# Sliding-window attention and adapter router: the transpose of the attention result by DMA instead of by TensorE and VectorE

## The chip, the cores and the metric

The kernel runs on one core of a Trainium2 chip. The metric is the device time of one execution in microseconds (us). The engines are PE (TensorE: matmuls; its weight loads are shown as PEld), ACT (ScalarE), DVE (VectorE), POOL (GpSimd) and SP (SyncE). POOL and SP do little here but issue DMAs, POOL the loads and SP the stores; 16 DMA engines move the data of both.

## The reference

q, k and v are float32 of shape 8 batches x 8 heads x 576 positions x 64. Each position attends to the positions at a distance of at most 32 in its own head. The result, laid out as 4608 rows of 512, is the input x of a router over 8 experts with adapters of rank 16; the best two experts add their adapter's output to the row.

```
scores = scale * np.matmul(q, k.transpose(0, 1, 3, 2))
mask = np.abs(pos[:, None] - pos[None, :]) <= window          # window = 32
attn = softmax(np.where(mask, scores, -1e9))                  # abridged
x = matmul(attn, v).transpose(0, 2, 1, 3).reshape(B * S, H * D)
...
logits = x @ w_gate                                           # K = 2 best of 8
for e in range(E):
    z = x[mask] @ A[e]                                        # 512 -> 16
    delta[mask] += w[mask, k, None] * (z @ B[e])              # 16 -> 512
return x + delta
```

## The kernel before, in words

Everything on the chip between the loads and the output is float16, with sums in float32 in PSUM. The unit of the attention is a pair of heads of one batch: 4 pairs a batch, 32 units u in all, each cut into 9 blocks of 64 keys. Eight blocks make one tile T of scores, 36 tiles in all.

Per batch b, the stages are these, each a small function named by two letters:

- LD and LV (L286, L290) load q, k (six loads) and v (two), issued by POOL, which casts them to float16 on the way. RG (L301) regroups q and k by a DVE copy; SV (L295) does v's.
- TR (L306) transposes q and k on PE, eight small matmuls against the identity for each of six pieces; EQ and EK (L315, L321) evict them by ACT.
- SC(T) (L328) computes a tile of scores into PSUM: two matmuls that write the mask and eight of q and k. EX(T) (L341) takes the exponential by ACT. PV(u) (L346) multiplies by v, 13 matmuls, with a column of ones that gives the sum. MU(u) (L359) divides by the sum on DVE: a reciprocal (L364) and a multiplication (L365) into the buffer x of the batch, 128 partitions x 5 groups x 512.
- When the four units of a batch are done, x must lie transposed. TX(b, h) (L372) does that on PE: 20 transposes of 128 x 128, in three parts h of 8, 8 and 4, into the PSUM buffers T. XE(b, h) (L381, the copy is L383) copies each part into xT on DVE.
- PZ(b) (L387, the matmul is L391) multiplies xT with the router's weights and all adapters' A, 20 matmuls. G1, GA, G2 (L400 to L431) pick the two best experts and scale on DVE, with one small exponential on ACT. TZ (L433) transposes the scaled result on PE and ZE (L439) evicts it on ACT.
- PD(b, h) (L443) forms the output in PSUM for the three parts h (256, 256 and 128 positions): the adapters' B (L446) plus x itself, by multiplying xT with the identity (L449). OB(b, h) (L453) evicts it to a float32 buffer ob, by ACT (L458) for h = 0 and 1 (128 x 1024) and by DVE (L460) for h = 2 (128 x 512). ST(b, h) (L462, the issue is L466) stores it from SP.

Buffers: x and xT have two copies each (NX, NXT), ob three (NOB), v three (NV), the raw loads seven pieces each of q and k (NRAW). PSUM is divided into three buffers W of 128 x 1024 float32 (NW; SC, PV, PZ and PD take them) and two buffers T of 128 x 1024 float16 (NTP; TR, TX and TZ take them).

The order of the instructions on every engine is fixed at build time. `tasks` (L64) lists each stage with its engine, its cost in us, what it depends on and which PSUM buffer it takes; every stage has a due time, counted in units u, which is its unit plus a number from the table OFF (L58). `plan` (L169) then places the tasks one by one in modelled time: on each engine, among the tasks that can start within `horizon` of the earliest, the one with the smallest due time. Loads have the engine "DMA" and stores the engine "DMO", and share one modelled transfer time; a task that depends on a load or a store waits `lat` (2.0 us) more. The kernel emits the stages in that order (L523) and keeps it (`keep` is the call that holds an instruction to its place in the program). At run time an engine works through its list in order and waits at each instruction for what it needs.

Of the kernel before, what the change touches and what calls it, by code (L numbers as in the profile page):

```python
# [16 lines left out]
B, H, S, D = 8, 8, 576, 64  # L17
E, R, DD = 8, 16, 512
ER = E * R
NP = H // 2  # L20
# [18 lines left out]
NV, NPT, NRAW, NCAST, NX, NXT, NOB = 3, 4, 7, 3, 2, 2, 3  # L39
# [9 lines left out]
class Task:  # L49
# [3 lines left out]
    def __init__(self, key, eng, cost, deps, take=None, give=None, lat=0.2):  # L53
# [1 line left out]
        self.take, self.give, self.lat = take, give, lat  # L55


OFF = {"LD": -10.16, "LV": -7.58, "RG": -2.51, "TR": -3.5, "EQ": -0.91, "EK": 8.24, "SV": 11.71,  # L58
       "SC": -2.02, "EX": 9.98, "PV": -0.24, "MU": -0.5, "TX": 0.38, "XE": -20.72, "PZ": 4.91,
       "G1": -40.48, "GA": 17.51, "G2": -27.59, "TZ": -20.47, "ZE": 17.82, "PD": 10.1, "OB": -2.95,  # L60
       "ZK": -28.38, "ZV": 29.47, "ZP": 16.04}


def tasks(off=OFF):  # L64

    ts = {}

    def add(key, u, eng, cost, deps, take=None, give=None, lat=0.2):
        t = Task(key, eng, cost, [d for d in deps if d in ts], take, give, lat)
        t.due = u + off[key[0]]  # L70
        t.seq = len(ts)
        ts[key] = t

    for i in range(2):
        for o in (0, 1):
            add(("ZK", i, o), -4.0 + 8 * i, "DVE", 1.05, [])
    for i in range(NPT):
        add(("ZP", i), -3.0 + i, "DVE", 0.56, [])
    for i in range(NV):
        for o in (0, 1):  # L80
            add(("ZV", i, o), 4 * i, "ACT" if i == 1 else "DVE", 2.2 if i == 1 else 1.2, [])

    def tiles_of(b):
        return range(NS * b // TB, (NS * b + NS - 1) // TB + 1)

    for b in range(B + 1):
        u0 = NP * b
        if b < B:
            for t in range(NT3):
                for w in (0, 1):  # L90
                    i = NT3 * b + t - NRAW
                    add(("LD", b, w, t), u0 + 1.333 * t, "DMA", 1.15,
                        [("RG", i // NT3, w, i % NT3)], lat=2.0)
            for o in (0, 1):
                add(("LV", b, o), u0 + o, "DMA", 1.8,
                    [("PV", NP * (b - NV) + n) for n in range(NP)], lat=2.0)
            for t in range(NT3):
                u = u0 + 1.333 * t
                for w in (0, 1):
                    i = NT3 * b + t - NCAST  # L100
                    add(("RG", b, w, t), u, "DVE", 0.43,
                        [("LD", b, w, t), ("TR", i // NT3, w, i % NT3)])
                for w in (0, 1):
                    add(("TR", b, w, t), u, "PE", 0.42, [("RG", b, w, t)], take="T")
                old = [("SC", T) for T in tiles_of(b - 2)] if b > 1 else []
                add(("EQ", b, t), u, "ACT", 0.80, [("TR", b, 0, t)] + old,
                    give=("TR", b, 0, t))
                add(("EK", b, t), u, "ACT", 1.60, [("TR", b, 1, t)] + old,
                    give=("TR", b, 1, t))
            for o in (0, 1):  # L110
                add(("SV", b, o), u0, "DVE", 0.78, [("LV", b, o)])

        for T in range(NT):
            last = TB * T + TB - 1
            if last // NS != b:
                continue
            need = set()
            for blk in range(TB * T, TB * T + TB + 1):
                bb, s = divmod(blk, NS)
                if bb < B and blk <= last:  # L120
                    need |= {("EQ", bb, s // BT), ("EK", bb, s // BT)}
                    if s % NB != NB - 1:
                        need.add(("EQ", bb, (s + 1) // BT))
                    need |= {("ZK", bb % 2, 0), ("ZK", bb % 2, 1)}
            u = (TB * T) / NB
            add(("SC", T), u, "PE", 0.90, list(need), take="W")
            pold = [("PV", v) for v in range(NU)
                    if NB * v < TB * (T - NPT) + TB and NB * v + NB > TB * (T - NPT)]
            add(("EX", T), u, "ACT", 1.03, [("SC", T)] + pold, give=("SC", T))
        us = [u for u in range(NU)  # L130
              if (NB * u + NB - 1) // TB in [T for T in range(NT) if (TB * T + TB - 1) // NS == b]]
        for u in us:
            bb = u // NP
            add(("PV", u), u, "PE", 0.80,
                [("EX", T) for T in range(NB * u // TB, (NB * u + NB - 1) // TB + 1)]
                + [("ZP", T % NPT) for T in range(NB * u // TB, (NB * u + NB - 1) // TB + 1)]
                + [("SV", bb, 0), ("SV", bb, 1), ("ZV", bb % NV, 0), ("ZV", bb % NV, 1)],
                take="W")
            add(("MU", u), u, "DVE", 1.05,
                [("PV", u)] + [("TX", bb - NX, h) for h in range(3)], give=("PV", u))  # L140
            if u % NP != NP - 1:
                continue
            v0 = NP * bb
            for h in range(3):
                n = 2 if h < 2 else 1
                add(("TX", bb, h), v0, "PE", 0.23 * n,
                    [("MU", v0 + i) for i in range(NP)], take="T")
                add(("XE", bb, h), v0, "DVE", 0.68 if n == 2 else 0.42,
                    [("TX", bb, h)] + [("PD", bb - NXT, i) for i in range(3)],
                    give=("TX", bb, h))  # L150
            add(("PZ", bb), v0, "PE", 1.2, [("XE", bb, h) for h in range(3)], take="W")
            add(("G1", bb), v0, "DVE", 1.08, [("PZ", bb)])
            add(("GA", bb), v0, "ACT", 0.22, [("G1", bb)])
            add(("G2", bb), v0, "DVE", 1.95, [("GA", bb)], give=("PZ", bb))
            add(("TZ", bb), v0, "PE", 0.30, [("G2", bb)], take="T")
            add(("ZE", bb), v0, "ACT", 0.70, [("TZ", bb)], give=("TZ", bb))
            for h in range(3):
                n = 2 if h < 2 else 1
                add(("PD", bb, h), v0 + 0.8 * h, "PE", 0.45 * n, [("ZE", bb)], take="W")
                k = 3 * bb + h - NOB  # L160
                add(("OB", bb, h), v0 + 0.8 * h, "ACT" if h < 2 else "DVE",
                    1.02 if n == 2 else 0.70, [("PD", bb, h), ("ST", k // 3, k % 3)],
                    give=("PD", bb, h))
                off["ST"] = off["OB"]
                add(("ST", bb, h), v0 + 0.8 * h, "DMO", 0.5 * n, [("OB", bb, h)], lat=2.0)
    return ts


def plan(off=OFF, horizon=0.036):  # L169

    ts = tasks(off)
    for t in ts.values():
        t.users, t.start = [], None
# [10 lines left out]
    n = len(ts)  # L184
    while len(order) < n:
# [45 lines left out]
        if t.give:  # L231
            g = ts[t.give]
# [11 lines left out]
def kernel(  # L244
# [10 lines left out]
    nc = tc.nc  # L255
    keep = tc.keep_in_program_order
# [6 lines left out]
    def many(n, shape, dt, name):  # L263
        return [const.tile(shape, dt, name=f"{name}{i}") for i in range(n)]
# [7 lines left out]
    xs = many(NX, [128, NG, DD], F16, "x")  # L272
    xTs = many(NXT, [128, NG, 4, 128], F16, "xT")
# [4 lines left out]
    Ts = [psum.tile([128, 1024], F16, name=f"T{i}") for i in range(NTP)]  # L278

    ts, order = plan()  # L280

    def ps(*key):
        t = ts[key]
        return (Ws if t.take == "W" else Ts)[t.slot]
# [96 lines left out]
    def XE(b, h):  # L381
# [2 lines left out]
            out=xTs[b % NXT][:, 2 * h:2 * h + n].rearrange("p g c k -> p (g c k)"),  # L384
            in_=ps("TX", b, h)[:, 0:512 * n]))

    def PZ(b):  # L387
        xT, pz = xTs[b % NXT], ps("PZ", b)
        for g in range(NG):
            for c in range(4):  # L390
                keep(nc.tensor.matmul(out=pz[:, GS * g:GS * g + ER + E],  # L391
                                 lhsT=xT[:, g, c, :], rhs=WA_sb[:, c, :],
                                 start=(c == 0), stop=(c == 3)))
# [68 lines left out]
    def ST(b, h):  # L462
        for i, g in enumerate(gs(h)):
# [1 line left out]
            r0 = S * b + 128 * g - 32  # L465
            keep(nc.sync.dma_start(out=out[r0 + lo:r0 + hi], in_=obs[(3 * b + h) % NOB][lo:hi, i]))  # L466

    do = dict(LD=LD, LV=LV, SV=SV, RG=RG, TR=TR, EQ=EQ, EK=EK, SC=SC, EX=EX, PV=PV, MU=MU,
              TX=TX, XE=XE, PZ=PZ, G1=G1, GA=GA, G2=G2, TZ=TZ, ZE=ZE, PD=PD, OB=OB, ST=ST)


# [92 lines left out]
```

## Time and profile before

| | us |
|---|---|
| three runs | 149.59, 150.68, 153.41 (median 150.68) |
| the profiled execution | 148.89 |
| its span, first to last instruction | 146.7 |
| busy: PE, ACT, DVE, POOL | 119.8, 116.3, 113.3, 51.9 |
| granted TensorE clock, mean | 0.979 |
| read from and written to HBM | 28.85 MB, 9.44 MB |

The views of the profile used below are: the page's slices, which cut the span into 40 equal parts and show the busy share of each in tenths; busy time by stretch, a row for each stretch of the span with the busy us of each engine and the number of its instructions; the groups by shape, with the line, engine and operation, the tiles written and read, the count, then busy us in all, ns of one, and after the second bar the engine's idle time just ahead of such instructions with what ended it; the waits, which name the waiting engine and line, then what it waited for, us in all, the number of times and the longest; the timeline, instructions in order with start and duration, and in brackets the idle time ahead; the chain of waits that ended last, with start, us and what; and the DMA issues, with the median us from issue to landing. An "L" with a number is a line of the kernel.

### The profile page before, as it was taken

The numbers are of one execution on the slowest core, as the hardware profiler recorded it, in microseconds if no ns is written. First come the engines' busy times: TensorE is split into PE (matmuls) and PEld (weight loads), VectorE is DVE, ScalarE is ACT, GpSimd is POOL, SyncE is SP. The second block draws the span as 40 slices with busy tenths as digits, with TensorE's granted clock in tenths as the row PEclk, the third lists the DMA queues.
The fourth block names the chain that finished last, engine by engine and source line by source line (L and its number), as shares of the span: only waits on it lengthen the run. The fifth ranks groups of instructions, "written<-read, shape, count | busy, mean of one in ns | idle before, by whom it ended". The sixth has DMA issues, their size and how long they took to land.

```text
span 146.7 us, 4230 instructions
## 1 busy us (share of the span) xinstructions
PE 119.8 (82%) x1720; PEld 100.8 (69%) x1720; DVE 113.3 (77%) x284; ACT 116.3 (79%) x143; POOL 51.9 (35%) x79
## 2 busy tenths in 40 slices
PE   0179779859889989878999999999999999693550
PEld 0156667649768978667789888997898788582330
DVE  6897899578997999975999999979738775967110
ACT  7789969948998899749999799989998994433150
POOL 7995657984576726610491044000000000000000
PEclk9999999999999999999999999999999999999686
DMA  2999999999999999999999959990542023058035
GB/s 20 179 157 179 196 191 95 163 150 180 205 191 194 225 226 195 235 264 241 257 177 206 249 104 125 227 238 8 197 179 93 0 58 130 0 201 290 32 136 186
DMA packets 38771, 24.13 MB, mean 164 GB/s; under 512 B 24800, under 2 KB 34144, under 8 KB 38752
## 3 DMA queue, kind: packets, MB, share of 16 engines
q0 software_dynamic: 33504, 14.43, 89.8%
q1 hardware_dynamic: 5248, 9.44, 18.6%
q8 instruction: 13, 0.21, 0.6%
q14 instruction: 6, 0.05, 0.1%
HBM read 28.85 MB, written 9.44 MB: 261 GB/s over the span
## 4 chain that ended last, share of the span: by engine, by line
PE 38%; DMA 21%; ACT 15%; DVE 11%; issue 6%; POOL 5%; SPq 0%; ACTq 0%; POOLq 0%; DVEq 0%
DMA vbd<-in_v_dram 12%; PE W L355 6%; ACT kT L325 5%; PE W L331 5%; DMA l<-in_q_dram 5%; ACT PT L342 5%; PE W L337 5%; PE W L446 5%; PE W L449 5%; DMA out_dram<-ob 4%; PE T L377 4%; PE W L391 4%; POOL l L288 3%; PE T L311 3%; ACT qT L317 3%
## 5 line engine op out<-in xcount | busy, mean ns | idle before, releaser
L342 ACT ACTIVATE PT<-W 128x1024 f16<-128x1024 f32 x36 | 36.9, 1025 | 6.3 <-PE W L337 5.4
L325 ACT COPY kT<-T 64x768 f16<-64x768 f16 x48 | 38.1, 794 | 1.7 <-PE T L311 1.3
L311 PE MATMUL T<-ident,c 96*128 96x96 f16 x384 | 24.0, 213 | 9.9 <-DVE c L303 8.0
L355 PE MATMUL W<-vbd,PT 128*128 128x130 f16 x416 | 29.1, 219 | 1.7 <-DVE vbd L298 0.8
L311 PEld LDWEIGHTS <-c 96*128 96x128 f16 x384 | 20.0, 101 | 11.7 <-DVE c L303 9.6
L365 DVE TENSOR_TENSOR x<-W,rc 128x640 f16<-128x640 f32 x32 | 26.4, 825 | 1.1
L355 PEld LDWEIGHTS <-PT 128*128 128x128 f16 x416 | 25.2, 97 | 2.2 <-issue 2.2
L337 PEld LDWEIGHTS <-kT 128*128 128x128 f16 x288 | 19.5, 99 | 9.2 <-issue 0.8
L458 ACT COPY ob<-W 128x1024 f32<-128x1024 f32 x16 | 16.1, 1012 | 9.5 <-PE W L449 6.0
L331 PE MATMUL W<-ident,mask 128*128 128x512 f16 x72 | 22.1, 390 | 1.5 <-DVE x L365 0.8
L303 DVE COPY c<-l 96x1024 f16<-96x1024 f16 x48 | 20.3, 450 | 3.3 <-DMA l<-in_q_dram 2.3
L293 POOL DMA_DIRECT2D vbd<-in_v_dram x16 | 13.5, 846 | 25.5 <-PE W L355 17.5
L337 PE MATMUL W<-qT,kT 128*128 128x128 f16 x288 | 22.5, 221 | 0.0
L317 ACT COPY qT<-T 128x768 f16<-128x768 f16 x24 | 19.1, 797 | 3.3 <-PE T L311 3.2
L288 POOL DMA_DIRECT2D l<-in_k_dram x24 | 15.8, 658 | 6.0 <-DVE rc L364 2.6
L288 POOL DMA_DIRECT2D l<-in_q_dram x24 | 16.2, 673 | 3.6 <-POOLq L548 0.9
L449 PEld LDWEIGHTS <-xT 128*128 128x128 f16 x160 | 12.9, 102 | 6.0 <-issue 1.5
L446 PE MATMUL W<-B_sb,zT 128*128 128x512 f16 x40 | 16.0, 400 | 1.2 <-ACT zT L440 0.8
L449 PE MATMUL W<-ident,xT 128*128 128x128 f16 x160 | 16.2, 226 | 0.0
L383 DVE COPY xT<-T 128x1024 f16<-128x1024 f16 (+1 forms) x24 | 13.7, 596 | 3.1 <-PE T L377 3.0
L377 PE MATMUL T<-ident,x 128*128 128x128 f16 x160 | 12.2, 219 | 2.3 <-DVE xT L383 1.8
L298 DVE COPY vbd<-vbd 32x2304 f16<-32x2304 f16 x16 | 12.3, 767 | 1.6 <-DMA vbd<-in_v_dram 1.2
(46 smaller groups left out, 113.1 us busy)
## 6 DMA issues: line engine op xcount, KB each, us to landing
out_dram<-ob SPq DMA_DIRECT2D x24, 256.0 KB, 4.2
l<-in_q_dram POOLq DMA_DIRECT2D x24, 192.0 KB, 8.6
l<-in_k_dram POOLq DMA_DIRECT2D x24, 192.0 KB, 8.9
vbd<-in_v_dram POOLq DMA_DIRECT2D x16, 288.0 KB, 9.0
out_dram<-ob SPq DMA_DIRECT2D x16, 192.0 KB, 3.7
WA_sb<-in_moe_A_dram POOLq DMA_DIRECT2D x4, 32.0 KB, 8.5
B_sb<-in_moe_B_dram POOLq DMA_DIRECT2D x1, 128.0 KB, 4.4
WA_sb<-in_moe_w_gate_dram POOLq DMA_DIRECT2D x1, 8.0 KB, 5.3
```

Source lines behind the costliest of these rows:

```text
L288: keep(nc.gpsimd.dma_start(out=raw[w][(NT3 * b + t) % NRAW], in_=src[FT * t:FT * t + FT]))
L303: keep(nc.vector.tensor_copy(out=cst[w][i % NCAST], in_=raw[w][i % NRAW].rearrange("p o (j d) -> p j o d", j=J)))
L311: keep(nc.tensor.matmul(out=tp[:, FT * slot:FT * slot + FT], lhsT=src[:, j, :], rhs=ident[0:FT, 0:FT], is_transpose=True, start=True, stop ...
L317: keep(nc.scalar.copy(out=qTs[b % 2][:, c0:c0 + J * FT].rearrange("p (f j) -> p f j", j=J), in_=ps("TR", b, 0, t)[:, 0:J * FT].rearrange(" ...
L325: keep(nc.scalar.copy(out=dst.rearrange("p a (r f j) -> p a r f j", r=2, j=4), in_=kt[64 * o:64 * o + 64]))
L331: keep(nc.tensor.matmul(out=p[:, i:i + 4], lhsT=maskT, rhs=bcast(ident, 1, 4), start=True, stop=False))
L337: keep(nc.tensor.matmul(out=p[:, i], lhsT=kTs[b % 2][:, NB * n + a, :], rhs=qTs[b % 2][:, c0:c0 + 128], start=False, stop=(i % 4 == 3)))
L342: keep(nc.scalar.activation(out=PTs[T % NPT][:, :, 64:192], in_=ps("SC", T).rearrange("p (i c) -> p i c", c=128), func=AF.Exp, scale=1.0 / ...
L355: keep(nc.tensor.matmul(out=po[:, GS * g:GS * g + 2 * VD], lhsT=PTs[T % NPT][:, sl, off:off + 128], rhs=rhs[:, :, V0 - 1:V0 + D], start=(i ...
L365: keep(nc.vector.tensor_tensor(out=xs[b % NX].rearrange("p g (h n d) -> p g h n d", h=2, n=NP)[:, :, :, n], in0=pog[:, :, :, 1:VD], in1=bc ...
L446: keep(nc.tensor.matmul(out=pd[:, i], lhsT=zTs[b % 2][:, g], rhs=B_sb, start=True, stop=False))
L449: keep(nc.tensor.matmul(out=pd[:, i, 128 * c:128 * c + 128], lhsT=xTs[b % NXT][:, g, c], rhs=ident, start=False, stop=(c == 3)))
```

## The change

For batches 0 to 6 the new stage XD replaces TX and XE: one DMA transpose, issued by SP, from the batch's buffer x to xT, both in SBUF. Batch 7 keeps TX and XE. XD goes into the plan as a task of the store queue with a cost of 2.6 us and the usual 2.0 us of latency; it depends on the four MU of its batch and on the PD of the batch two before, whose xT it overwrites. PZ depends on it, and so does MU two batches later, which overwrites x. In odd batches the eviction OB with h = 1 goes to DVE. The table OFF is new and horizon is 0, so that all engines' orders differ from before. The lines of XD, and of OB and the rest of the plan:

```
-            add(("MU", u), ..., [("PV", u)] + [("TX", bb - NX, h) for h in range(3)], give=("PV", u))
+            add(("MU", u), ..., [("PV", u)] + [("XD", bb - NX)], give=("PV", u))
...
+            if bb < B - 1:
+                add(("XD", bb), v0, "DMO", 2.6, [("MU", v0 + i) for i in range(NP)]
+                    + [("PD", bb - NXT, i) for i in range(3)], lat=2.0)
-            for h in range(3):
+            for h in range(3 if bb == B - 1 else 0):
                 n = 2 if h < 2 else 1
                 add(("TX", bb, h), ...)
                 add(("XE", bb, h), ...)
-            add(("PZ", bb), v0, "PE", 1.2, [("XE", bb, h) for h in range(3)], take="W")
+            add(("PZ", bb), v0, "PE", 1.2, [("XE", bb, h) for h in range(3)] + [("XD", bb)],
+                take="W")
...
-                add(("OB", bb, h), v0 + 0.8 * h, "ACT" if h < 2 else "DVE",
-                    1.02 if n == 2 else 0.70, ...)
+                add(("OB", bb, h), v0 + 0.8 * h, "ACT" if h < 2 - bb % 2 else "DVE",
+                    0.59 if n == 1 and h < 2 else 1.02 if h < 2 - bb % 2
+                    else 0.69 * n - 0.15 * (n - 1), ...)
...
-def plan(off=OFF, horizon=0.036):
+def plan(off=OFF, horizon=0):
...
+    def XD(b):
+        keep(nc.sync.dma_start_transpose(
+            out=xTs[b % NXT].rearrange("p g c k -> p (g c) k"),
+            in_=xs[b % NX].rearrange("p g c -> p (g c)")))
```

In the table OFF, of the stages around the change: PZ goes from 4.91 to -18.38, G1 from -40.48 to -46.69, G2 from -27.59 to -18.4, TZ from -20.47 to -7.62, PD from 10.1 to 14.0, OB (and with it ST) from -2.95 to 4.96, SC from -2.02 to 1.86, TR from -3.5 to -11.98, MU from -0.5 to -4.43; XD has -15.21.

## The prediction

> **What bounds the kernel now.** I read the clock and the DMA queues first, then the busy time by stretch, then the groups by shape, the waits and the timeline.
>
> ```profile
> PEclk9999999999999999999999999999999999999686
> DMA  2999999999999999999999959990542023058035
> ...
> q0 software_dynamic: 33504, 14.43, 89.8%
> q1 hardware_dynamic: 5248, 9.44, 18.6%
> ```
>
> The clock is full until the tail. q0, the loads that POOL issues, keeps the 16 DMA engines occupied to about 97 us; q1, the stores that SP issues, is light.
>
> ```profile
> core 0: us, PE busy (x) PEld busy (x) DVE busy (x) ACT busy (x) POOL busy (x), PEclk, DMA share, GB/s
> 20.00:30.00 10.00, 7.75 (x119) 6.42 (x118) 7.55 (x16) 8.79 (x12) 7.36 (x11) 1.00 3.20 143
> 70.00:80.00 10.00, 9.86 (x150) 8.46 (x149) 9.40 (x20) 9.93 (x13) 5.66 (x8) 1.00 1.33 211
> 80.00:90.00 10.00, 9.66 (x154) 8.47 (x152) 9.49 (x28) 9.21 (x14) 3.27 (x4) 1.00 1.02 166
> 90.00:100.00 10.00, 9.93 (x163) 8.86 (x161) 8.87 (x26) 9.40 (x13) 0.00 (x0) 1.00 1.06 194
> 130.00:140.00 10.00, 6.02 (x64) 4.38 (x62) 4.22 (x15) 3.27 (x5) 0.00 (x0) 0.85 0.42 145
> ```
>
> Three stages. To about 36 us nothing is full but the DMA. From 70 to 100 us PE is busy 29.45 of 30 us (98.2%), ACT 28.54 (95.1%), DVE 27.76 (92.5%): three engines nearly level, PE ahead. After 130 us the last batch's serial chain leaves all of them idle half the time.
>
> ```profile
> 26.39 0.82 DVE L365 TENSOR_TENSOR x<-W,rc 128x640 f16<-128x640 f32 x1
> 28.71 0.42 DVE L303 COPY c<-l 96x1024 f16<-96x1024 f16 x1 [1.50 <-DMA l<-in_q_dram]
> ...
> 44.72 0.75 DVE L298 COPY vbd<-vbd 32x2304 f16<-32x2304 f16 x1 [0.79 <-DMA vbd<-in_v_dram]
> ...
> 100.05 0.82 DVE L365 TENSOR_TENSOR x<-W,rc 128x640 f16<-128x640 f32 x1
> ...
> 127.76 0.82 DVE L365 TENSOR_TENSOR x<-W,rc 128x640 f16<-128x640 f32 x1
> ```
>
> The 4th L365 (batch 0 finished) starts at 26.39 us, the 32nd (batch 7) at 127.76: seven steps of 14.48 us. A gain per step counts seven times. Loads still hold DVE up at 28.71 and last at 44.72; later it is the other way round, POOL waits for a free V buffer (next fence, 17.5 us in two waits).
>
> ```profile
> POOL vbd L293 <- PE W L355: 17.5, 2, 9.0
> ...
> ACT ob L458 <- DMA out_dram<-ob: 3.5, 2, 2.9
> ```
>
> **The change, part by part.** The groups it touches, and the pitch of PE's transposes in the chain of waits:
>
> ```profile
> L458 ACT COPY ob<-W 128x1024 f32<-128x1024 f32 x16 | 16.1, 1012 | 9.5 <-PE W L449 6.0 <-DMA out_dram<-ob 3.5
> L377 PE MATMUL T<-ident,x 128*128 128x128 f16 x160 | 12.2, 219 | 2.3 <-DVE xT L383 1.8 <-ACT zT L440 0.4
> L383 DVE COPY xT<-T 128x1024 f16<-128x1024 f16 x16 | 10.8, 685 | 2.8 <-PE T L377 2.7
> L429 DVE TENSOR_TENSOR zs<-W,gate 128x640 f16<-128x640 f32 x8 | 6.6, 824 | 0.3
> L460 DVE COPY ob<-W 128x512 f32<-128x512 f32 x8 | 5.5, 690 | 5.4 <-PE W L449 5.0 <-ACT qT L317 0.3
> L383 DVE COPY xT<-T 128x512 f16<-128x512 f16 x8 | 3.3, 418 | 0.3 <-PE T L377 0.3
> ```
>
> ```profile
> 45.78 0.45 PE T L377 x8
> ```
>
> PE, removed. 140 of the 160 transposes (7 batches of 20). One lasts 219 ns but they overlap: 8 take 0.45 us, 56 ns each. 20 x 56 ns = 1.12 us a batch, 7.8 us in all.
> DVE, removed. Per batch 2 x 0.685 + 0.418 = 1.79 us, 12.5 us in all.
> DVE, added. The middle eviction (128x1024) of batches 1, 3, 5, 7. No DVE row has that shape. Two 128x512 copies would be 1.38 us (upper bound); ACT's 1.01 is the lower. 128x640 takes 0.824 and 128x512 0.690, 1.05 ns a column, so I take 0.690 + 512 x 1.05 ns = 1.23 us, near the upper row because it is the same engine. 4 x 1.23 = 4.9 us; net DVE -7.6 us.
> ACT, removed. 4 x 1.012 = 4.0 us; three of the four (3.0 us) lie in the steps, batch 7's in the tail.
> Effect on the steps. Occupied time per step is now 14.22 (PE), 13.77 (ACT), 13.40 us (DVE): the shares times 14.48. After: PE 14.22 - 1.12 = 13.10; ACT 13.77 - 3.0/6 = 13.27; DVE 13.40 - 1.79 + 3 x 1.23/6 = 12.2. ACT is then the fullest. If it fills as PE does now, a step is 13.27/0.982 = 13.51 us, 0.97 less, and seven give **-6.8 us**. Bounds: -3.0 (ACT's relief alone) and -7.8 (PE's whole relief).
> Tail. Batch 7's transposes stay. Its middle eviction goes to DVE, where the last one stands behind it:
>
> ```profile
> 141.04 1.01 ACT L458 COPY ob<-W 128x1024 f32<-128x1024 f32 x1 [0.37 <-PE W L449]
> ...
> 141.43 0.69 DVE L460 COPY ob<-W 128x512 f32<-128x512 f32 x1 [5.04 <-PE W L449]
> ```
>
> Started at 141.04, 1.23 us end at 142.27, and 0.69 more at 142.96, not 142.12: **+0.8 us** (0 if PE is done earlier).
> The DMA transposes, added. Seven of 128 x 2560 x 2 bytes = 655 KB, SBUF to SBUF, on SP's queue. No row shows one. By q1's own packet time (18.6% of 146.7 us for 9.44 MB, 346 GB/s) each occupies the DMA engines 1.9 us; by q0's (89.8%, 110 GB/s) 6.0. I take 1.9, since it is the queue SP issues on, and count it once: batch 0's transpose comes at 27 us, when compute waits for loads: **+1.9 us** (0 to 6.0). Batch 1's may cost the same again; from 45 us the loads have POOL's 17.5 us of idle waiting to give up, which is my cover for the others. Without it they would cost another 9.5 us.
>
> The Trainium skill's pages disagree on this price. "Advanced Engine Details and Errata", X-Bar Transpose (TRN2), holds that crossbar transposes move as fast as ordinary DMAs, 350 to 400 GB/s: an estimate of 1.6 to 1.9 us, which is the row's value. "VectorE: DVE Perf Modes", The three transpose paths, gives 1309 ns for one 128x128 block by DMA against 390 ns by TensorE: an estimate of 26 us for 20 blocks if they do not overlap. No run here shows either yet.
>
> Latency, moved. Transposing used to be PE, DVE, PE; now PE's first router matmul (L391) waits for a DMA. In the trace of before:
>
> ```profile
> 109.37 1.35 PE L391 MATMUL W<-WA_sb,xT 128*128 128x136 f16 x20
> ```
>
> ```profile
> L466 SPq DMA_DIRECT2D out_dram<-ob x40: 326/386/1106, 47.0 to 143.0; - x40
> ...
> DMA to landing us min/median/max: 2.0/3.9/7.9
> ```
>
> ```profile
> out_dram<-ob SPq DMA_DIRECT2D x24, 256.0 KB, 4.2
> ```
>
> It ran 8.5 us after batch 5 was finished (100.87). The new plan books 2.6 us plus 2.0 us, 4.6 us, for the transpose, and gives L391 a due time (-18.38) that puts it first on PE once the plan thinks it ready. What is later than 4.6 us stalls PE, with scores, PV and the next q/k transposes queued behind it. Bounds for the landing: 2.0 us (the fastest store) to 4.2 x 2.5 = 10.5 us (the median 256 KB store scaled to 655 KB). I take 4.6 and no stall: between far ends, an unloaded transfer is 2.0 + 393 KB/346 GB/s = 3.1 us, and PE's neighbours leave it some slack. What covers it is work the plan placed in between; if that is short, see rival one.
> SP's queue. One instruction more per batch, 0.39 us as for a store, at most 20 x 0.39 = 7.7 us if each block costs one. It waits for DVE's four L365; behind it stand stores. Their buffers come round after three evictions, so a late store shows as ACT waiting at L458, now 3.5 us. I price it at 0, since the output matmuls are due late in the new plan (PD at +14.0). MU of batch b+2 now waits for transpose b, a whole step of slack, 0.
> PSUM. The T buffers lose three users a batch; the 1.8 us that L377 waited for L383 goes, inside the gain above.
>
> Sum against the profiled execution's 148.89 us (span 146.7): 148.9 - 6.8 + 1.9 + 0.8 = **144.8 us**. That execution lies 0.7 below the fastest run shown (149.59) and 1.8 below the median (150.68); I forecast 145.5 for a run.
>
> **The rivals.**
> One, slower: PE waits at L391. Under load a transfer of 655 KB lands after 4.2 us + 393 KB at the mean rate of 164 GB/s (2.4) = 6.6 us.
>
> ```profile
> DMA packets 38771, 24.13 MB, mean 164 GB/s; under 512 B 24800, under 2 KB 34144, under 8 KB 38752
> ```
>
> That is 2.0 us over plan, seven times 14.0: 148.9 - 6.8 + 14.0 + 0.8 = 156.9. It decides from a lateness of 6.0/7 = 0.86 us, a landing 5.5 us after issue. For it: five of the seven transposes fall before 97 us, among the loads. Against it: after that the DMA engines are nearly free.
> Two, slower by far: short runs. The transpose reads 2560 runs of 128 elements. At q0's time per packet (131.7 us x 16 / 33504 = 63 ns) that is 10.1 us of all engines, landing after 12.1: 7.5 us late, 52 us in seven, 195 us. The Trainium skill's 26 us from the page on DVE perf modes would be worse still. For it: q0's packets are nearly as short (431 B). Against it: they read HBM and cast, a transpose does neither.
> Three, no change: ACT is already the limit. ACT is 99% busy from 70 to 80 us. Then only its 3.0 us count: 148.9 - 3.0 + 1.9 + 0.8 = 148.6. Against it: 92% in the next stretch. The transfer hidden but the gain lost to the new order comes to the same.
>
> **How the numbers follow.** Forecast 0.45, rival one 0.28, two 0.07, three 0.20. The forecast's own range is 141.8 (148.9 - 7.8, plus 0.7) to 148.6, where rival three takes over. The common range is 141.5 to 159: it leaves out rival two, rival one's upper part and a sliver below. About 2% is what a measurement of this kernel can tell from no change, 147.7 to 153.7 around the median. Faster by more: 0.43, the forecast but for its edge. Within: 0.22, rival three and the edges. Slower: 0.35, rivals one and two.
>
> **What would show it.** Right: steps of about 13.5 us between every fourth L365, ACT fuller than PE between 70 and 100 us, 20 matmuls and three copies left at L377 and L383, DVE evictions of 1.23 us, PE hardly waiting at L391. Wrong: PE idle at L391 released by the transpose (rival one above 0.86 us a batch); a landing over 10 us (two); ACT at 98% with PE well below and steps above 14 us (three); DVE waiting for loads after 45 us would mean that the transposes displace them. The prediction stands or falls with the transpose's time to landing, which nothing in this trace shows.

## The result and the profile after

The changed kernel takes 196.1 us (median of four runs, 195.23 to 200.34), the kernel before beside it 150.13 us: a ratio of 1.314 (95% interval 1.299 to 1.329). The forecast of 145.5 us and its range to 159 us are far off; rival two had said 195 us. (Ratios in this document compare undisturbed runs alone, medians take all, so that the two can differ by a percent or two.)

The profiled execution took 195.91 us, with a span of 194.1 us for 146.7 and a mean granted clock of 0.854 for 0.979. The page of the changed kernel, its slices, DMA queues, chain of work and the DMA issue of the transpose:

```profile
PEclk9999997885579755899955999559999999999797
DMA  4999999999999999469995499901992542882265
...
q1 hardware_dynamic: 23392, 14.03, 33.5%
...
DMA 51%; PE 21%; DVE 9%; issue 9%; ACT 4%; POOL 3%; DVEq 1%; POOLq 0%; ACTq 0%
...
xT<-x SPq DMA_TRANSPOSE x7, 12.5
```

q1 went from 5248 to 23392 packets: some 2590 for each of the seven transposes, 2560 of them rows of 128 elements. The DMA engines are busy, with two dips, to about 126 us and again to 146, not to 97. The chain was 21% DMA before and is 51% now. One part of it, in order of time (start, us, what):

```profile
32.33 20.18 DMA xT<-x
...
57.55 17.68 DMA xT<-x
...
87.72 15.61 DMA xT<-x
...
137.36 7.36 DMA xT<-x
...
166.38 5.97 DMA xT<-x
```

```profile
52.55 2.45 PE L400 MATMUL W<-WA_sb,xT 128*128 128x136 f16 x20 [13.61 <-DMA xT<-x]
...
144.76 1.36 PE L400 MATMUL W<-WA_sb,xT 128*128 128x136 f16 x20 [2.19 <-DMA xT<-x]
```

L400 is the router matmul that was L391 before; "DMA xT<-x" is the transpose. The first three take 20.2, 17.7 and 15.6 us, the fourth 12.5 (PE goes on at 124.90 for an issue at 112.36); the last two shown, when the loads are ending and over, 7.4 and 6.0. Behind waits of 13.6, 12.2, 10.2 and 7.2 us the 20 matmuls take 2.45 us; behind waits of 2.2 and 1.1 us they take 1.36: the clock that had been granted fell in the long waits (5 in the slices of PEclk). The waits and the transpose's own rows:

```profile
PE W L400 <- DMA xT<-x: 46.4, 6, 13.6
POOL vbd L297 <- PE W L359: 34.2, 2, 17.6
```

```profile
L392 SPq DMA_TRANSPOSE xT<-x x7: 2597/6282/11080, 32.3 to 166.4; - x7
...
DMA to landing us min/median/max: 4.1/12.5/20.2
```

PE's waits for the transpose add up to 46.4 us, and the span grew by 47.4. The loads' medians to landing, 8.9 and 9.0 us for q and k and 7.9 for v, are much as before. It looks as if the story were told: a late transfer and an engine that waits for it. The experiments say that this is where the loss shows and not all of what it is. The end of a batch's attention (every fourth L369), batches 0, 4 and 7, and of batch 4 in the kernel before:

```profile
31.48 0.82 DVE L369 TENSOR_TENSOR x<-W,rc 128x640 f16<-128x640 f32 x1
...
133.99 0.82 DVE L369 TENSOR_TENSOR x<-W,rc 128x640 f16<-128x640 f32 x1
...
171.69 0.82 DVE L369 TENSOR_TENSOR x<-W,rc 128x640 f16<-128x640 f32 x1
```

```profile
86.64 0.82 DVE L365 TENSOR_TENSOR x<-W,rc 128x640 f16<-128x640 f32 x1
```

Batch 0 ends 5.1 us later than before (31.48 for 26.39), ahead of the first transpose, which is the new order's doing. The four steps from batch 0 to 4 take 102.5 us (60.3 before, 26.39 to 86.64), the last three 37.7 (41.1 before). So the whole loss of 42 us lies in the steps in which loads are under way, and where there are hardly any left the steps are shorter than before.

### The profile page after: what moved, and what is told of

Its sections match the earlier page's. It is cut to its first block, busy times and chain, and to the rows that moved or that the text cites. A ratio compares the mean times of both kernels' runs of the same rounds, so it can differ in the third digit from the quotient of the medians.

```text
span 194.1 us, 3920 instructions
## 1 busy us (share of the span) xinstructions
PE 121.5 (63%) x1580; PEld 102.1 (53%) x1580; DVE 106.1 (55%) x267; ACT 112.4 (58%) x139; POOL 50.9 (26%) x79
## 3 DMA queue, kind: packets, MB, share of 16 engines
q1 hardware_dynamic: 23392, 14.03, 33.5%
## 4 chain that ended last, share of the span: by engine, by line
DMA 51%; PE 21%; DVE 9%; issue 9%; ACT 4%; POOL 3%; DVEq 1%; POOLq 0%; ACTq 0%
DMA xT<-x 38%; DMA l<-in_k_dram 8%; PE W L400 5%; DMA vbd<-in_v_dram 3%; PE W L359 3%; PE W L455 3%; PE W L458 3%; PE W L335 2%; PE W L341 2%; POOL l L292 2%; DVE x L369 2%; ACT PT L346 2%; PE T L315 1%; DVE ob L469 1%; DVE zs L438 1%
## 5 line engine op out<-in xcount | busy, mean ns | idle before, releaser
L400 PE MATMUL W<-WA_sb,xT 128*128 128x136 f16 x160 | 15.2, 271 | 46.5 <-DMA xT<-x 46.4
L346 ACT ACTIVATE PT<-W 128x1024 f16<-128x1024 f32 x36 | 36.4, 1034 | 13.3 <-issue 10.7
L400 PEld LDWEIGHTS <-xT 128*128 128x128 f16 x160 | 13.5, 122 | 47.6 <-DMA xT<-x 47.4
L359 PE MATMUL W<-vbd,PT 128*128 128x130 f16 x416 | 31.4, 231 | 5.5 <-DVE vbd L302 5.4
L315 PE MATMUL T<-ident,c 96*128 96x96 f16 x384 | 26.9, 220 | 8.8 <-DVE c L307 7.4
L417 DVE TENSOR_REDUCE m<-W 128x5 f32<-128x40 f32 x8 | 1.6, 200 | 55.4 <-PE W L400 55.4
L359 PEld LDWEIGHTS <-PT 128*128 128x128 f16 x416 | 27.8, 104 | 6.0 <-DVE vbd L302 3.5
L315 PEld LDWEIGHTS <-c 96*128 96x128 f16 x384 | 22.3, 106 | 9.6 <-DVE c L307 8.0
L369 DVE TENSOR_TENSOR x<-W,rc 128x640 f16<-128x640 f32 x32 | 26.4, 824 | 1.1
L335 PE MATMUL W<-ident,mask 128*128 128x512 f16 x72 | 23.0, 403 | 0.7 <-DVE ob L469 0.4
L292 POOL DMA_DIRECT2D l<-in_q_dram x24 | 15.4, 644 | 8.2 <-DVE c L307 4.8
L458 PE MATMUL W<-ident,xT 128*128 128x128 f16 x160 | 16.2, 226 | 0.0
L458 PEld LDWEIGHTS <-xT 128*128 128x128 f16 x160 | 12.8, 101 | 5.7 <-issue 1.2
L467 ACT COPY ob<-W 128x1024 f32<-128x1024 f32 x12 | 12.2, 1016 | 6.0 <-PE W L458 4.7
## 6 DMA issues: line engine op xcount, KB each, us to landing
xT<-x SPq DMA_TRANSPOSE x7, 12.5
```

Of the source, the lines that this page charges most:

```text
L292: keep(nc.gpsimd.dma_start(out=raw[w][(NT3 * b + t) % NRAW], in_=src[FT * t:FT * t + FT]))
L315: keep(nc.tensor.matmul(out=tp[:, FT * slot:FT * slot + FT], lhsT=src[:, j, :], rhs=ident[0:FT, 0:FT], is_transpose=True, start=True, stop ...
L335: keep(nc.tensor.matmul(out=p[:, i:i + 4], lhsT=maskT, rhs=bcast(ident, 1, 4), start=True, stop=False))
L346: keep(nc.scalar.activation(out=PTs[T % NPT][:, :, 64:192], in_=ps("SC", T).rearrange("p (i c) -> p i c", c=128), func=AF.Exp, scale=1.0 / ...
L359: keep(nc.tensor.matmul(out=po[:, GS * g:GS * g + 2 * VD], lhsT=PTs[T % NPT][:, sl, off:off + 128], rhs=rhs[:, :, V0 - 1:V0 + D], start=(i ...
L369: keep(nc.vector.tensor_tensor(out=xs[b % NX].rearrange("p g (h n d) -> p g h n d", h=2, n=NP)[:, :, :, n], in0=pog[:, :, :, 1:VD], in1=bc ...
```

## The experiments

### What keeps the transposes late

Is it the plain amount of data (bytes theory), the many small packets beside those of the loads (turns theory), or the new order of the work (plan theory)? The first run replaces the transpose:

```
-        keep(nc.sync.dma_start_transpose(
-            out=xTs[b % NXT].rearrange("p g c k -> p (g c) k"),
+        keep(nc.sync.dma_start(
+            out=xTs[b % NXT].rearrange("p g c k -> p (g c k)"),
```

> The changed kernel, but each of the seven transposes is a plain copy of the same 655 KB from x to xT in the same place of SP's queue (xT then holds x untransposed, so the router and the output are computed from the wrong layout; all other work is the same). Turns theory: the transpose is late because its 2560 packets of 256 bytes take turns with the packets of the loads; the copy moves rows of 5120 bytes in a fraction of the packets, lands within 4 to 9 us beside the loads, PE waits at L400 for less than 12 us in all and the time is 148 to 160 us. Bytes theory: the DMA engines are full and any 655 KB put beside the loads comes late; landing stays at 12 to 20 us and the time at 185 to 196 us. Plan theory: the new order is what costs; the time stays above 185 us even if the copy lands early.

Measured: 156.81 us (one run, before 150.8). PE waits 10.9 us at L400, and the copies land so:

```profile
L392 SPq DMA_DIRECT2D xT<-x x7: 464/471/2120, 32.9 to 127.3; - x7
...
  PE W L400: 10.9, 6
...
DMA to landing us min/median/max: 3.2/7.0/9.1
```

The bytes theory and the plan theory fall as accounts of the bulk of the loss: same order, same bytes, 39 us less. A copy in long rows still lands 7.0 us after issue in the median, more than the 4.6 that the plan books.

The second run takes the loads away from the changed kernel:

```
+        if t.key[0] == "LD" and NT3 * t.key[1] + t.key[3] >= NRAW or t.key[0] == "LV" and t.key[1] >= NV:
+            continue
         do[t.key[0]](*t.key[1:])
```

> The changed kernel without the q and k loads after the seventh piece of each and without the v loads of batches 3 to 7 (later batches compute on what is in the buffers). Turns and bytes theory: the transposes of batch 2 and later land in 4 to 6 us, PE's waits of 10.2, 7.2 and 2.2 us at L400 for batches 2 to 4 go, those of batches 0 and 1 stay in part; 160 to 175 us. Plan theory: 185 us or more, with PE still waiting in the later batches.

Measured: 141.35 us (one run), under every theory's figure, since the first two transposes went free as well.

```profile
L392 SPq DMA_TRANSPOSE xT<-x x7: 2461/2586/4136, 32.1 to 112.3; - x7
...
  PE W L400: 1.6, 2
...
DMA to landing us min/median/max: 4.1/4.2/6.2
```

With no load beside it the transpose lands in 4.2 us, under the 4.6 booked, and PE waits 1.6 us in all. The same edit in the kernel before gives what the change is worth there:

> The kernel before without the q and k loads after the seventh piece of each and without the v loads of batches 3 to 7, as the changed kernel was run at 141.35 us. It prices the change where the transposes meet no loads. By the forecast's own step of 6.8 us less 0.8: 146 to 149 us; if the change is worth nothing there, 141 to 143 us.

Measured: 146.15 us (one run), so the change gains 4.8 us (3.3%) where the transposes meet no loads. Between the end of batch 0 and that of batch 7, without the loads, first changed and then before:

```profile
31.24 0.82 DVE L369 TENSOR_TENSOR x<-W,rc 128x640 f16<-128x640 f32 x1
...
117.61 0.82 DVE L369 TENSOR_TENSOR x<-W,rc 128x640 f16<-128x640 f32 x1
```

```profile
28.01 0.82 DVE L365 TENSOR_TENSOR x<-W,rc 128x640 f16<-128x640 f32 x1
...
125.07 0.82 DVE L365 TENSOR_TENSOR x<-W,rc 128x640 f16<-128x640 f32 x1
```

12.34 us a step for 13.87, 10.7 us in seven; batch 0 ends 3.2 us later and the tail is 3.0 us longer, so that 4.5 us of the span are left. The granted clock was 0.996 in the one and 0.964 in the other, so part of these 1.5 us may be the chip's and not the change's.

### Is it the wait, or what the transposes do to the loads?

The kernel before, with its own order and PE's transposes, and the DMA transposes beside them into a buffer that nobody reads:

```
+    sp = many(1, [128, NG, 4, 128], F16, "sp")
...
         do[t.key[0]](*t.key[1:])
+        if t.key[0] == "MU" and t.key[1] % NP == NP - 1 and t.key[1] < NU - 1:
+            keep(nc.sync.dma_start_transpose(
+                out=sp[0].rearrange("p g c k -> p (g c) k"),
+                in_=xs[t.key[1] // NP % NX].rearrange("p g c -> p (g c)")))
```

> The kernel before, with its own order and its transposes on PE, and beside them the seven DMA transposes into a spare buffer that nobody reads (batch b + 2 overwrites x only after its transpose has landed). Turns theory: the transposes of batches 0 to 3 again land after 12 to 20 us and the last two after 4 to 6, but nothing waits for them; what they take from the loads falls into the time that POOL waits for V buffers, so 150 to 155 us. Bytes theory: the loads are pushed back by 6 us for each of the first five, 160 us or more. Plan theory: as the kernel before, 149 to 151 us, and landings of 4 to 7 us throughout.

Measured: 189.77 us, a ratio of 1.272 (1.262 to 1.281), 39 us more. The turns theory and the plan theory had it that nobody would be hurt; the bytes theory is right in kind, that the loads are pushed back, but by more than its 6 us a transfer. Its chain, its DMA issues and two of its waits:

```profile
DMA vbd<-in_v_dram 54%; PE W L356 3%; PE W L392 3%; PE W L447 3%; PE W L450 3%; POOL l L289 3%; PE W L338 2%; PE T L378 2%; PE W L332 2%; PE T L312 2%; ACT kT L326 1%; ACT qT L318 1%; DVE zs L430 1%; DVE ob L461 1%; PE T L437 1%
```

```profile
l<-in_q_dram POOLq DMA_DIRECT2D x24, 192.0 KB, 15.5
...
vbd<-in_v_dram POOLq DMA_DIRECT2D x16, 288.0 KB, 15.4
...
sp<-x SPq DMA_TRANSPOSE x7, 16.9
```

```profile
DVE vbd L299 <- DMA vbd<-in_v_dram: 27.7, 7, 9.3
...
ACT ob L459 <- DMA out_dram<-ob: 16.1, 2, 15.4
```

```profile
96.64 1.01 ACT L459 COPY ob<-W 128x1024 f32<-128x1024 f32 x1 [15.43 <-DMA out_dram<-ob]
```

The loads now land after 15 us for 8.6 to 9.0 before, and they, not the transposes, are the chain. So transposes and loads hold each other up, and the kernel pays for the loads even when no compute engine waits for a transpose.

The loads are not the whole price in this run. SP's queue has the stores too, and behind the third transpose, issued at 73.60, one of them lands so late that ACT stands 15.4 us, to 96.64, for the output buffer that it frees. The step in which that falls, batch 2 to 3, takes 35.2 us for 16.2 in the profiled execution (194.19 us); the steps to batches 1, 2 and 5 are 9.6, 3.9 and 12.5 us longer than before. Part of that wait belongs to this experiment: one spare buffer serves all transposes, and the third is issued only when the second has landed (52.66 + 20.9 us).

Two transposes alone, to see whether POOL's waits for V buffers make good what they take:

```
-... and t.key[1] < NU - 1:
+... and t.key[1] < 2 * NP:
```

> The kernel before with spare transposes of batches 0 and 1 alone. Five beside the loads cost 39 us, 8 us each; two would be 16 us. If POOL's 17.5 us of waiting for V buffers cover that, as the prediction held, the time is 151 to 155 us; if the loss comes before those waits and is not made good, 160 to 168 us.

Measured: 163.82 us, a ratio of 1.090 (1.074 to 1.105), 12 us more, as expected of a loss that is not made good. Here ACT waits only 0.5 us for stores, so this price is that of the loads:

```profile
DVE vbd L299 <- DMA vbd<-in_v_dram: 9.0, 3, 8.3
...
POOL vbd L294 <- PE W L356: 6.2, 1, 6.2
```

POOL's waits for V buffers did shrink, from 17.5 to 6.2 us, but the time that DVE lost before, waiting for late loads, did not come back. The changed kernel with L400 planned later asks the question from the other side:

```
-                    + [("PD", bb - NXT, i) for i in range(3)], lat=2.0)
+                    + [("PD", bb - NXT, i) for i in range(3)], lat=6.0)
```

> The changed kernel with the transpose's booked latency at 6 us for 2, so that the plan puts L400 some 4 us later and other work ahead of it. If PE's wait at L400 is a loss of its own, six waits shrink by up to 4 us each: 172 to 180 us. If the loads that the transposes hold up are the loss, and the wait at L400 is only where it shows, PE waits elsewhere instead: 188 to 198 us.

Measured: 186.25 us (two runs), a ratio of 1.245 (1.237 to 1.252). Some 10 us come back, between the two expectations, and the transposes land later still:

```profile
PE W L400 <- DMA xT<-x: 35.3, 4, 11.5
POOL vbd L297 <- DMA vbd<-in_v_dram: 22.1, 7, 6.7
```

```profile
DMA to landing us min/median/max: 4.4/19.8/23.1
```

So the wait at L400 has a price of its own, about 10 us for 11 us of waiting less. The larger part of the loss, 36 us, stays, but with 35.3 us of waiting at L400 in it and 22.1 us at POOL for loads (9.1 in the changed kernel), so this run alone does not part the two.

### Small packets, or the transposing?

The spare transfer in the kernel before, once as a plain copy in rows of 256 bytes and once in rows of 5120:

```
+    sp = many(1, [128, NG * 4, 144], F16, "sp")
...
+            keep(nc.sync.dma_start(out=sp[0][:, :, 0:128], in_=xs[...].rearrange("p g (c k) -> p (g c) k", k=128)))
```

```
+    sp = many(1, [128, NG, 512], F16, "sp")
...
+            keep(nc.sync.dma_start(out=sp[0].rearrange("p g c -> p (g c)"), in_=xs[...].rearrange("p g c -> p (g c)")))
```

> The kernel before with a spare transfer per batch that nobody reads, as in the run with spare transposes (189.8 us), but a plain copy in rows of 256 bytes (the spare buffer has a gap after every 128 elements). Packet theory: the loads lose their turns to 2560 small packets whatever these do; the copies land after 12 to 17 us beside the loads and the time is 180 to 195 us. Crossbar theory: it is the transposing that holds other traffic up; the copies land in 4 to 10 us and the time is 150 to 158 us.

> The same with a plain copy in rows of 5120 bytes. Both theories: 0 to 6 us above the kernel before (150.8), since seven transfers of 655 KB are only 4.6 of its 24.1 MB; if bytes were the price, each would take 6 us from the loads and the time would be 160 us or more.

Measured: 166.91 us (two runs; ratio 1.107, 1.089 to 1.126) in short rows and 156.86 us (1.030, 1.015 to 1.044) in long ones, beside 189.77 us for the transposes; 15, 5 and 39 us more than before. The packets of the run with short rows, then the landings, short rows and long:

```profile
q1 hardware_dynamic: 23280, 14.03, 33.3%
```

```profile
DMA to landing us min/median/max: 4.9/12.9/16.5
```

```profile
DMA to landing us min/median/max: 3.6/7.5/9.1
```

Neither theory alone holds. The short rows make as many packets as the transposes (23280 on q1, 23392 there) and cost 10 us more than the long ones; the transposing costs another 23 us. The stretches in which the second spare transfer runs, transposed, in short rows, in long rows (the last column is GB/s):

```profile
44.00:52.00 8.00, 2.12 (x23) 2.12 (x23) 5.45 (x19) 3.40 (x5) 3.02 (x5) 0.50 1.48 179
57.00:70.00 13.00, 9.98 (x162) 8.81 (x160) 8.82 (x26) 9.24 (x13) 3.47 (x5) 1.00 1.38 108
```

```profile
50.00:61.00 11.00, 10.04 (x160) 8.81 (x159) 9.71 (x28) 9.34 (x13) 4.76 (x8) 1.00 1.32 193
```

```profile
48.00:51.00 3.00, 3.00 (x45) 2.53 (x43) 2.94 (x7) 2.59 (x3) 1.96 (x3) 1.00 1.18 286
```

The first row is the stretch of loads alone ahead of the transpose, 179 GB/s; ahead of the second copy of either kind the loads move 196. The queues' rows (packets, MB, share of the 16 engines) in the stretches of the transpose and of the short rows:

```profile
q1 hardware_dynamic: 2574, 0.70, 85.0%
q0 software_dynamic: 1160, 0.70, 52.7%
```

```profile
q0 software_dynamic: 2482, 1.33, 84.8%
q1 hardware_dynamic: 2550, 0.77, 46.3%
```

While the transpose runs, the 16 engines move 108 GB/s in all, and the loads' queue has 54 of them (0.70 MB in 13 us), a third of what it had. Beside the short rows it keeps 121 for 11 us, beside the long rows 70 (0.21 MB), but for 3 us. A packet of the transpose lasts 69 ns there (85.0% of 16 x 13 us, by 2574), one of the short rows 32 ns, and the loads' packets 94 ns beside the one and 60 beside the other. Where the transposes meet no loads, their queue's packets last 21 ns (2698 packets in 82.2% of 16 x 4.24 us, a few of them of stores, in the changed kernel without the loads).

What the loads lose, an estimate from these rates: 13 x (1 - 54/179) = 9.1 us a transpose, 11 x (1 - 121/196) = 4.2 us a copy in short rows, 3 x (1 - 70/196) = 1.9 us in long. Five of the seven meet loads: 45, 21 and 10 us, in the order of the 39, 15 and 5 us measured. The sizes can't be held against each other closely, since part of the measured loss came by the stores, with the short rows as with the transposes:

```profile
ACT ob L459 <- DMA out_dram<-ob: 11.6, 2, 10.7
```

That wait lies in the step from batch 2 to 3, which takes 28.4 us for 16.2, 12 us more; the other steps grow by 2.7 us at most. Why the transposing halves what all engines move together was not tried further and stays open.

### A version that beats both

If holding up loads is the price, transposes belong behind the loads. Three were tried first:

```
+XDL = {4: 8, 5: 4, 6: 4}                # batch: booked latency
...
-            if bb < B - 1:
+            if bb in XDL:
```

> DMA transposes for batches 4, 5 and 6 alone, where the loads are nearly done; batches 0 to 3 and 7 are transposed on PE. The plan books 2.6 us plus 8 us for batch 4 and plus 4 us for batches 5 and 6, its due times are chosen anew; odd batches' middle eviction stays on VectorE. Turns and bytes theory: landings under 11, 7 and 7 us, PE hardly waits, and PE, VectorE and ScalarE are relieved in three batches: 143 to 147 us. Plan theory: no faster than before, 150 us or more.

Measured: 147.99 us beside 150.8 (ratio 0.977, 0.970 to 0.984), a little above the 143 to 147 expected. The first of the three still met loads and landed after 13.3 us. With batches 5 and 6 alone (XDL = {5: 4, 6: 4}), and then the same due times with all batches on PE (XDL = {}):

> DMA transposes for batches 5 and 6 alone, booked at 2.6 + 4 us, the due times chosen anew; the others are transposed on PE and odd batches' middle eviction stays on VectorE. Holding up loads is the price of a transpose, and here the loads are over: landings of 4 to 7 us, no waits at L400, 143 to 146 us, better than the 148.0 us of the run with batches 4 to 6, whose first transpose still met loads. If the transposes' price were in the waiting, it would be no better than that run.

> The same due times as the run with DMA transposes of batches 5 and 6, but with every batch transposed on PE. If that run gains by its two transposes, this one is 3 to 5 us slower, 148 to 151 us; if it gains by its new order alone, the two are level.

Measured: 146.57 us for batches 5 and 6 (median; 149.85 before; ratio 0.956, 0.947 to 0.964) and 150.41 us with all on PE (ratio 0.990, 0.984 to 0.995). All six times of the one (141.99 to 147.09) lie below all thirteen of the other (147.47 to 153.4), so the two transposes gain: 3.8 us by the medians, 3.4% by the ratios. The size is loose, since the 0.956 rests on two of the six runs, and the median lies just above the 143 to 146 expected. The new due times with the moved eviction, which both have, are worth 1%.

```profile
L392 SPq DMA_TRANSPOSE xT<-x x2: 2492/2558/2624, 103.7 to 118.0; - x2
...
DMA to landing us min/median/max: 4.5/5.2/5.9
```

The loads of this run end before 103.7 us, and nothing waits at L400.

## Why the prediction was wrong, point by point

- What bounds the kernel: right as far as it went. From 70 to 100 us three engines are level, and relieving them shortens the steps where no loads are under way (12.34 us, forecast 13.51). What was missed is that until batch 4 the loads are part of the bound: without them the kernel before takes 56.0 us and not 60.3 from batch 0 to 4, and 41.1 as ever from 4 to 7. The rows stood in the prediction: the DMA slices full to 97 us, and DVE waiting for loads as late as 44.72.
- PE, DVE and ACT removed, DVE added: right. L381 has 20 matmuls left, and the moved eviction takes 1222 ns, forecast 1.23. Without loads the seven steps gain 10.7 us for the 6.8 forecast, part of it perhaps the clock's. (The forecast spread the evictions that leave ACT over six steps and counted seven; spread over seven it would have been 6.3.)

```profile
L469 DVE COPY ob<-W 128x1024 f32<-128x1024 f32 x4 | 4.9, 1222 | 2.7 <-PE W L458 2.6
...
L381 PE MATMUL T<-ident,x 128*128 128x128 f16 x20 | 1.4, 219 | 0.9 <-DVE xT L387 0.9
```

- The tail, +0.8: it is 3.5 us longer (171.69 to 194.1 for 127.76 to 146.7), and 3.0 us longer without the loads too (22.0 for 19.0). The changed kernel also ends batch 0 later, by 5.1 us and, without the loads, by 3.2. No run takes the moved eviction and the new order apart; what goes beyond the 0.8 was not in the sum, which took the replanning at nothing.
- The DMA transposes, +1.9 once: this is the step that failed. The term took a transfer by its bytes and the fast queue's rate. Alone that holds (4.2 us to landing). Beside the loads the first four take 12 to 20 us and in the stretch measured the loads fall to a third; seven cost 39 us, by way of loads and stores, in the run in which no compute engine waits for them. The upper end, 6.0 us each, was counted for one transpose, and the cover given for the others, POOL's 17.5 us of waiting, covers only in part: those waits lie after 62 us, and the two transposes before that cost 12 us although the waits shrank to 6.2.
- The landing taken at 4.6 us and no stall: wrong for the same reason; 12.5 us in the median and 46.4 us of waiting. This is rival one's place with rival two's size. The point from which lateness decides, 5.5 us, is not tested: the plain copies that PE waits for land after 7.0 us and give 156.81 us, by rival one's working 6.6 and 156.9, but copies that no compute engine waits for cost 5 us too.
- SP's queue at 0: right for the changed kernel as far as waits go, where no eviction waits for a store (ACT 3.5 us before). But the issue takes up to 11.1 us, over the upper bound of 7.7, and in two of the runs with spare transfers ACT stands 15.4 and 10.7 us for a store behind one.
- Rival two: its landing (12.1 us against 12.5) and time (195 against 196.1) came out, its mechanism only half. It made 10 us of DMA time from 2560 short packets at the loads' packet time. That price holds for the transposes beside loads (69 ns a packet, forecast 63), not for short rows (32 ns, 15 us in all and not 50), and not for transposes without loads (21 ns): the shortness alone doesn't make it. The total agrees in part by luck, since it had seven equal stalls of 7.5 us and the trace has six, from 13.6 down to 1.1. What was sound in it is that it was built on the row of a queue under load, where the forecast was built on that of a quiet one.
- The pages: "VectorE: DVE Perf Modes", The three transpose paths, of the Trainium skill would make 26 us of 20 blocks, an estimate; the runs show 4.2 us with no other traffic. "Advanced Engine Details and Errata", X-Bar Transpose (TRN2), of the Trainium skill has transposes as fast as ordinary DMAs; the runs agree for a quiet chip (4.1 us at the least against 3.2 for the plain copy) and not beside loads (16.9 against 7.5 in the median).

## What to carry to other kernels

A DMA that is moved onto a shared set of engines is priced by what it meets there, and by what it takes from the others: read the queue's share at the time it will run, and take the rate of the busy queue, not of the quiet one. Look too at what stands behind it in its own queue, here the stores. An idle wait of the issuing engine is not a full reserve: what other engines have lost before it, waiting for late loads, does not come back. A DMA transpose goes where the loads are over, and a spare one that nobody reads, put into the old kernel, shows its price in one run.

## What the runs showed of the hardware that was not expected

- A DMA transpose of 128 x 2560 two-byte elements lands in 4.2 us on quiet engines and in 12 to 23 us in the thick of the loads, and in the stretch measured all 16 engines together move 108 GB/s where the loads alone had moved 179.
- A plain copy of the same bytes with as many packets leaves the total at 193 GB/s. The transposing costs more than its packets.
- SP is held too: the transpose's issue takes 2.5 to 2.6 us on quiet engines and up to 11.1 us beside loads, a plain copy's 0.47 to 0.61 in the median. Stores behind either can land late: ACT waited 15.4 and 10.7 us for one.
- After waits of 7.2 to 13.6 us the clock granted to TensorE is halved for a while: the 20 router matmuls take 2.45 us and not 1.36. After waits of 2.2 and 1.1 us it is not.
